# Half of the columns of two query-weight loads read from a source laid out in four spaced groups of 32 rows

## The chip, the cores and the metric

The kernel runs on one core of one Trainium2 chip. The metric is the device time of one execution in microseconds. A core has TensorE (PE in the profile; its weight loads are PEld), VectorE (DVE), ScalarE (ACT), GpSimd (POOL) and SyncE (SP). SP only issues transfers here. Sixteen DMA engines move the data between the device's memory (HBM) and the on-chip memory, SBUF, which has 128 partitions.

## The reference

The program is one decode step of a model with two layers, each an attention block and a token-mixing block, with the same weights and the same cache in both layers. All numbers are float32; the batch is 2, the width 512, with 32 query heads and 8 key/value heads of 128, and a cache of 32768 positions.

```python
B, Sq, D = 2, 1, 512
Hq, Hkv, Sk, Dh = 32, 8, 32768, 128
...
q = (x @ wq).reshape(B, Sq, Hq, Dh).transpose(0, 2, 1, 3)
scores = einsum("bhqd,bhkd->bhqk", q, repeat(k_cache, 4)) * Dh ** -0.5
o = einsum("bhqk,bhkd->bhqd", softmax(scores), repeat(v_cache, 4))
attention = o.transpose(0, 2, 1, 3).reshape(B, Sq, Hq * Dh) @ wo
...
x = x + attention(layernorm(x));  x = x + mixer(layernorm(x))     # layer 0
x = x + attention(layernorm(x));  x = x + mixer(layernorm(x))     # layer 1
```

The mixer is `w2` times gelu of `w1` times the normalised row, with a hidden size of 1792. The cache of one batch row and one key/value head is 16 MB of keys and 16 MB of values. There are 16 such pairs, and each is read once for each layer, except for a part that the kernel keeps between the layers.

## The kernel before

**Tiles.** `mem` is one large SBUF buffer, cut into 106 cells of 128 partitions x 512 columns (256 KB each). Keys, values and the weights `wq` and `wo` of a head all land in cells. A load fills 1 to 32 neighbouring cells; a weight load fills 4 cells (128 x 2048, 1024 KB).

**Units and steps.** A unit is (layer, batch row, head). It has a K phase of 64 cells (`k_step`, the products on L360, which make scores) and a V phase of 64 cells (`v_step`, L428, which makes the weighted sum of the values). A step is four cells. `Order` writes the order of all phases: K of one unit stands between V of the units before it, so that the softmax of a unit is done beside products of others. At the change of layers (twice, once for each batch row) the program has to finish a row's attention, its mixer and its normalisation before the first query of layer 1 for that row exists. Other units' phases fill that time. What lies before those two changes is the first long stretch (layer 0, to about 1000 us), and what lies behind them the second (layer 1, from about 1500 us).

**Queries.** `wide_products` (L325) multiplies the normalised rows with `wq` of one head, four products of 512 columns, one for each fourth of the 2048 columns of the load. `make_q` does this ten steps ahead of the unit's K phase. PE takes its instructions in one order, and a product that waits for its weights holds all that stand behind it.

**Loads.** `plan_loads` runs before the program is built. It walks the steps with estimated times, decides for each load how many cells it takes and which, and after which step SP issues it. A weight load for a query is asked for 16 steps ahead of its K phase. All loads of keys, values and weights are issued by SP, in one queue, in that order (L885 for keys and values, L880 for weights); SP waits until the products that read the cells' old content are done, and then issues. A transfer's landing is told by one of eight semaphores, taken in turn (DMAHW0 to DMAHW7 in the rows below); it counts to 16 when all parts of the transfer have landed. PE waits on that semaphore before it reads the cells. ACT issues two small loads at the start and one store of a single row of the output (L592); the last store (L757) is issued by SP.

**Sources.** The host lays the inputs out so that a load is 128 rows, one for each partition: `wqo[h]` has 128 rows, each with the 2048 columns of `wq` and then the 2048 of `wo`.

```python
part, layer, h = u
w = D * R
at_w = 0 if part == "q" else w
nc.sync.dma_start(cells(a, n), wqo[h][:, at_w : at_w + w])
```

Of the kernel before, what the change touches and what calls it, by code (L numbers as in the profile page):

```python
# [13 lines left out]
P = 128  # L14
# [24 lines left out]
STEP_US = 1.6  # L39
ASK_Q = 16  # L40
ASK_O = 8


class Order:
# [158 lines left out]


@with_exitstack
def gqa_mixer_kernel(ctx: ExitStack, tc: tile.TileContext, x, kt, v, wqo, cols, out):
    nc = tc.nc
    B, D = out.shape
    HKV = wqo.shape[0]
# [21 lines left out]
    def cells(a, n):  # L231
        return mem[:, a * G : (a + n) * G]
# [541 lines left out]
    for u in order.units:  # L774
        layer, b, h = u
# [11 lines left out]
    for name, us in users.items():  # L787
        k0 = min(first["K", u] for u in us)
        h = name if isinstance(name, int) else name[1]
# [3 lines left out]
        weights.append((k0 - ASK_Q if k0 else -1, ("q", layer, h), max(first["K", u] for u in us) if both else k0))  # L793
        weights.append((k0 if both else v0 + ASK_O, ("o", layer, h), max(end["V", u, 1] for u in us) + 3))

    for u in order.units:
        layer, b, h = u
# [76 lines left out]
    def load(label, n, a):  # L874
        kind, u, g = label
        if kind == "W":
            part, layer, h = u
            w = D * R
            at_w = 0 if part == "q" else w
            nc.sync.dma_start(cells(a, n), wqo[h][:, at_w : at_w + w])  # L880
            (wq_sb if part == "q" else wo_sb)[layer, h] = cells(a, n).rearrange("p (t c) -> p t c", t=DT)
            return
        layer, b, h = u
        src = (kt if kind == "K" else v)[b * HKV + h, g // HALF, :, (g % HALF) * G : (g % HALF + n) * G]
        nc.sync.dma_start(cells(a, n), src)  # L885
        for j in range(n):
            at_cell[kind, u, g + j] = a + j
            if (kind, u, g + j) in order.kept:
                at_cell[order.kept[kind, u, g + j]] = a + j
# [5 lines left out]
    for label, n, a in begin.get(-1, ()):  # L895
        load(label, n, a)
# [4 lines left out]
    for p, (kind, u, g) in enumerate(steps):  # L901
        (k_step if kind == "K" else v_step)(u, g)
        for f, args in hooks.pop(p, ()):
            f(*args)
        for label, n, a in begin.get(p, ()):
            load(label, n, a)
# [3 lines left out]
def _layout(A_x, A_k_cache, A_v_cache, A_wq, A_wo, B_w1, B_b1, B_w2, B_b2):  # L910
    import numpy as np

    B, HKV, SK, DH = A_k_cache.shape
    D = A_x.shape[-1]
    U = B * HKV
    kt = A_k_cache.reshape(U, 2, NG, 32, 2, 2, 8, 2, 2, DH).transpose(0, 1, 9, 4, 7, 8, 2, 5, 6, 3)
    wq = A_wq.reshape(D // P, P, HKV, -1).transpose(2, 1, 0, 3)
    wo = A_wo.reshape(HKV, -1, DH, D).transpose(0, 2, 1, 3)
    w1, b1, w2 = (a.reshape(P, -1) for a in (B_w1, B_b1, B_w2))
    none = np.zeros_like(w2)  # L920
    w2z = np.stack([none, w2], axis=2).reshape(P, -1)
    cols = [w1, b1, w2z, none[:, :1], np.broadcast_to(B_b2.reshape(1, 1), (P, 1))]
    return {
        "x": np.ascontiguousarray(A_x.reshape(B * (D // P), P).T),
        "kt": np.ascontiguousarray(kt).reshape(U, 2, DH, HALF * G),
        "v": A_v_cache.reshape(U, 2, P, HALF * G),
        "wqo": np.concatenate([wq.reshape(HKV, P, -1), wo.reshape(HKV, DH, -1)], axis=2),
        "cols": np.concatenate(cols, axis=1),
    }


_INS = ["x", "kt", "v", "wqo", "cols"]


# [20 lines left out]
```

## Time and profile before

| | |
|---|---|
| median of 3 runs | 2499.34 us (2498.99 to 2500.09) |
| the profiled execution's own time | 2498.83 us |
| its span in the trace | 2497.0 us |
| PE busy | 1339.3 us, 54% of the span |
| DVE, ACT, POOL busy | 211.4, 186.9 and 5.1 us |
| read from HBM | 1063.29 MB |
| mean rate of the DMA engines | 426 GB/s |
| SP's transfer queue (q1) | 99.1% of the time of 16 engines |

The span goes from the first instruction to the last; the execution's own time has some 2 us around it. The busy time of an engine is a sum over its instructions. The DMA row of the profile is a mean over 16 engines: 1.00 means that each of them had a packet under way at all times, and 0.50 that they were busy half of the time on average. PE waits for data for most of its idle time, so the question for any change here is which of the 16 engines ends last, and when.

### The profile page before, as it was taken

The numbers are of one execution on the slowest core, as the hardware profiler recorded it, in microseconds if no ns is written. First come the engines' busy times: TensorE is split into PE (matmuls) and PEld (weight loads), VectorE is DVE, ScalarE is ACT, GpSimd is POOL, SyncE is SP. The second block draws the span as 40 slices with busy tenths as digits, with TensorE's granted clock in tenths as the row PEclk, the third lists the DMA queues.
The fourth block names the chain that finished last, engine by engine and source line by source line (L and its number), as shares of the span: only waits on it lengthen the run. The fifth ranks groups of instructions, "written<-read, shape, count | busy, mean of one in ns | idle before, by whom it ended". The sixth has DMA issues, their size and how long they took to land.

```text
span 2497.0 us, 21065 instructions
## 1 busy us (share of the span) xinstructions
PE 1339.3 (54%) x9562; PEld 374.6 (15%) x9562; DVE 211.4 (8%) x600; ACT 186.9 (7%) x581; POOL 5.1 (0%) x18
## 2 busy tenths in 40 slices
PE   3445454444445544556676774554444544554567
PEld 1111111111111111111121221111111111111113
DVE  1000000000000000101110110000000000000012
ACT  0100000000000000001110210000000000000021
POOL 0000000000000000000000000000000000000000
PEclk8777777777777777778887986777777777777688
DMA  9999999999999999999999999999999999999996
GB/s 421 434 436 430 432 432 433 430 430 436 435 430 432 430 432 434 426 436 408 417 425 423 421 427 435 434 434 430 430 437 423 439 431 435 433 433 430 432 430 277
DMA packets 34947, 1064.64 MB, mean 426 GB/s; under 512 B 4134, under 2 KB 4138, under 8 KB 5035
## 3 DMA queue, kind: packets, MB, share of 16 engines
q1 hardware_dynamic: 34568, 1063.27, 99.1%
q8 instruction: 75, 1.23, 0.2%
q14 instruction: 14, 0.11, 0.0%
q10 hardware_dynamic: 290, 0.04, 0.0%
HBM read 1063.29 MB, written 0.00 MB: 426 GB/s over the span
## 4 chain that ended last, share of the span: by engine, by line
DMA 63%; PE 24%; another core or an unknown queue 11%; DVE 1%; issue 0%; ACT 0%; SPq 0%; POOLq 0%; POOL 0%; DVEq 0%; ACTq 0%
DMA mem<-in_v_dram 35%; DMA mem<-in_kt_dram 29%; PE acc L428 13%; PE scores L360 8%; PE misc L332 1%; PE bcast L325 0%; PE rows L492 0%; PE misc L384 0%; PE misc L657 0%; PE misc L451 0%; DVE row L462 0%; PE misc L378 0%; ACT S L410 0%; PE misc L471 0%
## 5 line engine op out<-in xcount | busy, mean ns | idle before, releaser
L428 PE MATMUL acc<-mem,S 128*16 128x512 f32 x4080 | 596.8, 719 | 586.9 <-DMA mem<-in_v_dram 578.6
L360 PE MATMUL scores<-mem,qz 128*32 128x512 f32 x4096 | 600.0, 727 | 538.4 <-DMA mem<-in_kt_dram 538.2
L410 ACT ACTIVATE S<-S,neg 128x128 f32<-128x128 f32 x256 | 129.6, 509 | 2213.8 <-DVE S L405 1188.7
L360 PEld LDWEIGHTS scores<-mem,qz 128*32 128x32 f32 x4096 | 142.5, 126 | 917.6 <-issue 827.0
L428 PEld LDWEIGHTS acc<-mem,S 128*16 128x16 f32 x4080 | 127.6, 107 | 903.5 <-issue 814.5
L370 DVE TENSOR_REDUCE mx<-scores 128x1 f32<-128x512 f32 x64 | 44.3, 691 | 801.3 <-PE scores L360 793.5
L405 DVE STREAM_TRANSPOSE S<-scores 128x512 f32<-128x512 f32 x64 | 45.5, 710 | 126.1 <-PE acc L428 126.1
L410 ACT ACTIVATION_READ_ACCUMULATOR S<-S,neg 128x1 f32 x256 | 47.7, 186 | 0.0
L492 PE MATMUL rows<-mem,oz 128*2 128x512 f32 x248 | 41.1, 744 | 0.3 <-DVE oz L481 0.3
L380 DVE TENSOR_REDUCE m<-misc 1x4 f32<-1x128 f32 x32 | 8.9, 279 | 380.8 <-PE misc L378 380.8
L453 DVE RECIPROCAL rl<-misc 128x4 f32<-128x4 f32 x32 | 5.8, 183 | 382.1 <-PE misc L451 382.1
L462 DVE SCALAR_TENSOR_TENSOR row<-acc,quad,row 128x128 f32<-128x128 f32 x96 | 33.6, 350 | 3.4
L460 DVE TENSOR_SCALAR row<-acc,quad 128x128 f32<-128x128 f32 x32 | 11.2, 351 | 170.3 <-PE acc L428 170.3
L481 DVE TENSOR_TENSOR oz<-misc,rl 128x4 f32<-128x4 f32 x32 | 5.2, 162 | 227.2 <-PE misc L471 226.7
L471 PEld LDWEIGHTS misc<-head,row 128*128 128x128 f32 x64 | 14.0, 274 | 52.2 <-issue 38.3
L325 PE MATMUL bcast<-mem,xw 128*32 128x512 f32 x144 | 20.0, 618 | 1.7 <-POOL x_rs L298 1.7
L471 PE MATMUL misc<-head,row 128*128 128x4 f32 x64 | 16.9, 334 | 7.3 <-DVE row L462 7.3
L451 PEld LDWEIGHTS misc<-both,one 128*128 128x128 f32 x64 | 12.9, 251 | 50.1 <-issue 47.2
L332 PEld LDWEIGHTS misc<-selg,row 128*128 128x128 f32 x128 | 17.1, 208 | 18.2 <-DVE rl L453 8.7
L576 ACT ACTIVATE row<-bcast,bias,scale 128x512 f32<-128x512 f32 x21 | 16.3, 777 | 37.8 <-PE rows L560 17.0
L378 PE MATMUL misc<-ident,mxa 128*1 128x128 f32 x64 | 18.1, 379 | 2.0 <-DVE mxa L376 2.0
L332 PE MATMUL misc<-selg,row 128*128 128x2 f32 (+1 forms) x128 | 18.5, 267 | 0.8 <-DVE row L317 0.8
(128 smaller groups left out, 278.1 us busy)
## 6 DMA issues: line engine op xcount, KB each, us to landing
mem<-in_v_dram SPq DMA_DIRECT2D x13, 4096.0 KB, 25.1
mem<-in_v_dram SPq DMA_DIRECT2D x37, 1024.0 KB, 9.1
mem<-in_kt_dram SPq DMA_DIRECT2D x15, 2048.0 KB, 17.9
mem<-in_kt_dram SPq DMA_DIRECT2D x30, 1024.0 KB, 10.3
mem<-in_wqo_dram SPq DMA_DIRECT2D x28, 1024.0 KB, 38.1
mem<-in_kt_dram SPq DMA_DIRECT2D x6, 4096.0 KB, 28.2
mem<-in_kt_dram SPq DMA_DIRECT2D x2, 6144.0 KB, 23.1
mem<-in_v_dram SPq DMA_DIRECT2D x3, 2048.0 KB, 38.8
```

Of the source, the lines that this page charges most:

```text
L325: nc.tensor.matmul(q_ps[us][32 * d : 32 * d + 32, :], xw[:, d, :], wq[:, d, :], start=True, stop=True)
L332: nc.tensor.matmul(pt[:, r * n : (r + 1) * n], q_row[us][:, r * DH : (r + 1) * DH], side, start=True, stop=True,)
L360: nc.tensor.matmul(sc_ps[u, half][32 * row : 32 * row + 32, :], qz[:, at : at + 32], cells(at_cell["K", u, g], 1), start=(i == 0), stop=(i ...
L370: nc.vector.tensor_reduce(mx[u][:, half : half + 1], sc_ps[u, half], axis=AX.X, op=ALU.max)
L378: nc.tensor.matmul(pm[:1, :P], mxa, ident, start=True, stop=True)
L405: nc.vector.transpose(S[half], sc_ps[u, half])
L410: nc.scalar.activation(s[:, :, h], s[:, :, h], AF.Exp, bias=neg[u][:, h : h + 1], scale=SCALE, accum_out=lsum[u][:, half, h : h + 1],)
L428: nc.tensor.matmul(acc[32 * row : 32 * row + R * QT, :], S[half][:, col : col + R * QT], vc, start=(g < NG), stop=(g >= quads - NG),)
L462: nc.vector.scalar_tensor_tensor(asb[u], acc[:, t * DH : (t + 1) * DH], quad[:, t : t + 1], asb[u], op0=ALU.mult, op1=ALU.add)
L471: nc.tensor.matmul(po_of[u][:, :R], asb[u], head, start=True, stop=(u != order.last))
L492: nc.tensor.matmul(rows[32 * r : 32 * r + B, :], oT[u][:, 2 * r + 1 - b : 2 * r + 3 - b], wo_of(u)[:, r, :], start=False, stop=(u == order ...
L576: nc.scalar.activation(hid[key, f], px[key], AF.Gelu_apprx_tanh, bias=shift[key][:, f : f + 1], scale=slope[key][:, f : f + 1],)
```

## The change

Two of the 28 weight loads are cut in two: `wq` of head 3 in layer 0 and `wq` of head 2 in layer 1. The left half (1024 of 2048 columns) is still read from `wqo`, as 128 rows. The right half is read from a new input, `narrow`. It holds the same numbers for each of the two loads, as four groups of 32 rows of 1024 columns, and behind each group stands one unused row of zeros, so that the four groups can't be written as 128 evenly spaced rows. The source pattern is then 4 groups x 32 rows x 1024 columns, and its slowest dimension is 4, where that of all other loads is 128. The destination is the right half of the columns of the same cells, 128 partitions. The bytes moved are the same, and no other load or instruction is changed.

```diff
+NARROW = (("q", 0, 3), ("q", 1, 2))
+NARROW_COLS = 1024
+NARROW_GROUPS = 4
...
-            nc.sync.dma_start(cells(a, n), wqo[h][:, at_w : at_w + w])
+            if u in NARROW:
+
+                cut = w - NARROW_COLS
+                nc.sync.dma_start(cells(a, n)[:, :cut], wqo[h][:, at_w : at_w + cut])
+                nc.sync.dma_start(cells(a, n)[:, cut:], narrow[NARROW.index(u)][:, : P // NARROW_GROUPS, :])
+            else:
+                nc.sync.dma_start(cells(a, n), wqo[h][:, at_w : at_w + w])
...
+    narrow = np.zeros((len(NARROW), NARROW_GROUPS, P // NARROW_GROUPS + 1, NARROW_COLS), np.float32)
+    for i, (part, _, h) in enumerate(NARROW):
+        w = (wq if part == "q" else wo)[h].reshape(NARROW_GROUPS, P // NARROW_GROUPS, -1)
+        narrow[i, :, :-1] = w[:, :, -NARROW_COLS:]
```

SP's queue at the first of the two loads, before. The names are the destination and the source, then the destination's sizes, and in brackets the semaphores that SP waits for ahead of the issue.

```order
L885 DMA mem<-in_kt_dram 128x16384 [waits DMAHW6_49,DMAHW1_49,PE_49]
L885 DMA mem<-in_kt_dram 128x16384 [waits DMAHW7_49,PE_49]
L880 DMA mem<-in_wqo_dram 128x2048 [waits DMAHW3_49]
L885 DMA mem<-in_v_dram 128x16384 [waits DMAHW0_49,PE_49]
L880 DMA mem<-in_wqo_dram 128x2048 [waits PE_49]
L885 DMA mem<-in_v_dram 128x16384 [waits DMAHW1_49,PE_49]
```

The same place after the change.

```order
L894 DMA mem<-in_kt_dram 128x16384 [waits DMAHW7_49,PE_49]
L886 DMA mem<-in_wqo_dram 128x1024 [waits DMAHW3_49]
L887 DMA mem<-in_narrow_dram 128x1x1024
L894 DMA mem<-in_v_dram 128x16384 [waits DMAHW0_49,PE_49]
L889 DMA mem<-in_wqo_dram 128x2048 [waits PE_49]
L894 DMA mem<-in_v_dram 128x16384 [waits DMAHW1_49,PE_49]
```

One row has become two, and the second waits for nothing of its own. The second load, `wq` of head 2 in layer 1, changes in the same way: it stands behind two loads of keys and ahead of a load of values there too. All loads behind the new one keep their order and take the next semaphore in turn.

PE at the products that read the first of these loads, before. In a row of L325 stand the products of the rows (`xw`) with the weights in `mem`, one for each fourth of the columns; `acc` is the weighted sum of values.

```order
L428 MATMUL acc<-mem,S_91 16x512 x12
L325 MATMUL bcast<-mem,xw 32x512 [waits DMAHW3_49]
L325 MATMUL bcast<-mem,xw 32x512 x3
L428 MATMUL acc<-mem,S_91 16x512 x4
L428 MATMUL acc<-mem,S_92 16x512 [waits DMAHW6_49,Activation_49]
```

The same place after the change.

```order
L431 MATMUL acc<-mem,S_91 16x512 x12
L328 MATMUL bcast<-mem,xw 32x512 [waits DMAHW3_49]
L328 MATMUL bcast<-mem,xw 32x512
L328 MATMUL bcast<-mem,xw 32x512 [waits DMAHW4_49]
L328 MATMUL bcast<-mem,xw 32x512
L431 MATMUL acc<-mem,S_91 16x512 x4
L431 MATMUL acc<-mem,S_92 16x512 [waits DMAHW7_49,Activation_49]
```

The last two of the four products now wait for the new transfer's own semaphore. DVE, ACT and POOL have the same rows as before.

More of the change, by code (lines that the diff above doesn't have):

```diff
@@ L205, in gqa_mixer_kernel @@
 @with_exitstack
-def gqa_mixer_kernel(ctx: ExitStack, tc: tile.TileContext, x, kt, v, wqo, cols, out):
+def gqa_mixer_kernel(ctx: ExitStack, tc: tile.TileContext, x, kt, v, wqo, narrow, cols, out):
     nc = tc.nc
@@ L927, in _layout @@
         "wqo": np.concatenate([wq.reshape(HKV, P, -1), wo.reshape(HKV, DH, -1)], axis=2),
+        "narrow": narrow,
         "cols": np.concatenate(cols, axis=1),
     }
-_INS = ["x", "kt", "v", "wqo", "cols"]
+_INS = ["x", "kt", "v", "wqo", "narrow", "cols"]
 def kernel(A_x, A_k_cache, A_v_cache, A_wq, A_wo, B_x, B_w1, B_b1, B_w2, B_b2):
```

## The prediction

> **What bounds the kernel now.** I read the page first: the DMA rows, the queues and the chain of waits.
>
> ```profile
> span 2497.0 us, 21065 instructions
> ...
> DMA  9999999999999999999999999999999999999996
> ...
> q1 hardware_dynamic: 34568, 1063.27, 99.1%
> q8 instruction: 75, 1.23, 0.2%
> ...
> DMA 63%; PE 24%; another core or an unknown queue 11%; DVE 1%; issue 0%; ACT 0%; SPq 0%; POOLq 0%; POOL 0%; DVEq 0%; ACTq 0%
> ```
>
> SP's queue (q1) fills 99.1% of the time of 16 engines. PE's 24% of the chain lies between landings, while the next loads are under way. So the kernel ends when the last DMA engine has moved its share, plus a tail. The second queue matters below: q8 carries the code of PE, 75 packets in 1.23 MB, so 16.4 KB each; 0.2% of 16 x 2497 us is 80 us, so about 1.07 us of one engine for each packet.
>
> The chain in order of time shows the end.
>
> ```profile
> 2398.86 41.45 DMA mem<-in_v_dram
> 2440.31 0.02 issue
> 2440.33 39.32 DMA mem<-in_v_dram
> 2479.65 0.04 issue
> 2479.70 0.45 PE held L437 x8
> ...
> 2493.94 0.35 DVE mem L756
> ```
>
> The last load of values lands at 2479.65 us and PE starts 0.05 us later. Behind it is a fixed tail of 17.4 us. Whatever the last landing gains or loses, the kernel gains or loses.
>
> Then the busy time by windows, for the two long stretches, the two changes of layer between them, and the last 14 us. The last two columns are the mean busy share of the 16 engines and their GB/s.
>
> ```profile
> 300.00:1000.00 700.00, 346.72 (x2411) 93.49 (x2412) 47.09 (x131) 35.88 (x136) 0.00 (x0) 0.73 1.00 432
> 1600.00:2400.00 800.00, 403.10 (x2830) 109.44 (x2822) 58.14 (x163) 51.94 (x174) 0.54 (x1) 0.75 1.00 433
> ...
> 1100.00:1260.00 160.00, 99.97 (x732) 28.13 (x736) 19.35 (x59) 24.79 (x60) 1.08 (x2) 0.84 0.99 415
> 1260.00:1480.00 220.00, 155.69 (x1170) 44.29 (x1166) 28.46 (x81) 26.86 (x68) 1.08 (x2) 0.84 1.01 425
> ...
> 2470.00:2472.00 2.00, 1.98 (x20) 0.67 (x24) 0.00 (x0) 0.00 (x0) 0.00 (x0) 1.00 1.01 414
> 2472.00:2474.00 2.00, 2.00 (x20) 0.60 (x12) 0.00 (x0) 0.00 (x0) 0.00 (x0) 1.00 0.66 268
> 2474.00:2476.00 2.00, 1.39 (x17) 0.40 (x17) 0.00 (x0) 0.00 (x0) 0.00 (x0) 1.00 0.49 205
> 2476.00:2478.00 2.00, 2.00 (x47) 1.41 (x40) 1.25 (x4) 0.00 (x0) 0.00 (x0) 1.00 0.50 198
> 2478.00:2480.00 2.00, 1.77 (x43) 0.85 (x35) 0.15 (x1) 0.00 (x0) 0.00 (x0) 1.00 0.19 69
> ```
>
> This is what to see: in the stretches all 16 engines work (1.00), but at the end the share falls to 0.66, stays at 0.5 for some 5 us and then goes to nothing. Half of the engines are done 5 to 7 us ahead of the other half. All have moved the same bytes of q1, since every large load is cut over 16 engines. Something else has held back eight.
>
> What it is, the completion marks tell: each transfer's semaphore is raised once by each engine. No view prints them; these are read from the trace behind the profile (issue, last mark, and how far ahead of it the other marks came, in us).
>
> ```
> issued    last mark   ahead of it by
>    2.12     65.27     1.9 1.8 1.7 1.6 1.6 1.6 1.6 1.6 1.5 1.5 1.5 1.4 1.4 1.1 1.0
>  358.34    405.82     3.6 3.3 3.2 3.1 2.8 2.7 2.7 2.3 1.8 1.8 1.8 1.7 1.6 1.5 0.1
>  943.07    973.09     6.7 6.3 6.3 5.8 5.6 5.3 5.2 4.4 1.8 1.7 1.7 1.7 1.6 1.5 0.1
> 1868.20   1916.77     3.8 3.6 3.5 3.5 3.3 3.0 2.8 2.7 1.4 1.3 0.5 0.3 0.3 0.3 0.1
> 2440.33   2479.65     7.1 6.9 6.8 6.8 6.6 6.3 5.3 5.1 1.7 0.8 0.6 0.6 0.5 0.4 0.3
> ```
>
> Eight engines run ahead more and more along a stretch, and lose part of that lead at the changes, where they run dry while the others work on. The other eight fall back one at a time, by about 1.5 us, and this happens at each packet of q8. So PE's code is fetched by eight of the engines in turn, and those eight end last.
>
> By the Trainium skill (Runtime: NRT & Kernel Launch, "Instruction fetch mechanics"), the code comes in blocks of 16 KiB through a DMA queue of the sequencer, and crossing a block is "mostly hidden". The block's size agrees with 16.4 KB a packet. That it is hidden does not hold for the engines that carry it: half of them are late by 5 to 7 us in the last windows.
>
> **The change part by part.** The unit price is 433 GB/s over 16, 27.1 GB/s an engine. A weight load of 1024 KB is 64 KB an engine, 2.42 us. If the new half goes over four engines, one of these two loads gives:
> - twelve engines 32 KB instead of 64: -1.21 us;
> - four engines 32 + 128 = 160 KB: +3.63 us.
>
> The rows are of 4 KB where they were 8 KB. The trace has no such long run of 4 KB rows. Bounds: nothing, or twice the loss that the first change of layer shows against the stretch with its rows of 8 KB (1 - 415/433, 4%), so 8%: 0.1 us on 32 KB and 0.5 us on 160 KB. I take the middle: -1.15 and +3.85 us.
>
> Now the question is which four. The engines that end last get -1.15 if they are not among them. The four then end last only where their lead is below 3.85 us. The one narrow transfer ahead of the end in this kernel is ACT's store of a single row:
>
> ```profile
> L592 ACTq DMA_DIRECT2D out_dram<-row x1: 505/505/505, 2409.3 to 2409.3; - x1
> ```
>
> Its packet of 2 KB, at 2413.84 us, stands in a gap of just one engine's packets in the trace, and that engine's marks are 6.6 us ahead. So the first engine that a narrow transfer takes is a leader. For the other three no row tells. By the Trainium skill (DMA: Bandwidth & Descriptors, "Why a DMA increments its semaphore by 16 and not by 1") a transfer runs on the largest number up to 16 that divides the slowest dimensions of both sides, here 4 of 4 and 128, and on the lowest-numbered engines. No view here shows those numbers.
>
> First stretch, if all four are leaders: right behind the load (marks at 405.82, leads of 2.3 to 3.6 us) they fall behind by up to 1.5 us. That costs nothing, because two more loads stand in their queues. Until 973 us they gain it back: of the eight leads seven are 5.2 or more and one is 4.4. The gain at the stretch's end is 1.15, or 4.4 - 3.85 = 0.55 if the slowest leader is among the four: I take 1.1 us. It goes through the changes whole, as the eight late engines have no idle time there (shares of 0.99 and 1.01, with the leaders' gaps in them). Second stretch: the smallest lead at the last landing is 5.1, more than 3.85, so the gain is 1.15 us.
>
> What the two products of L325 wait for is next. The load is issued right behind a load of keys, at both places:
>
> ```profile
> 358.34 0.33 SPq L885 DMA_DIRECT2D mem<-in_kt_dram  x1
> 358.72 0.42 SPq L880 DMA_DIRECT2D mem<-in_wqo_dram  x1
> 376.38 0.33 SPq L885 DMA_DIRECT2D mem<-in_v_dram  x1
> ...
> 358.34 47.48 DMA mem<-in_kt_dram
> ...
> 436.53 1.04 PE L325 MATMUL bcast<-mem,xw 128*32 128x512 f32 x8
> ...
> 1868.20 0.33 SPq L885 DMA_DIRECT2D mem<-in_kt_dram  x1
> 1868.58 0.42 SPq L880 DMA_DIRECT2D mem<-in_wqo_dram  x1
> 1887.83 0.33 SPq L885 DMA_DIRECT2D mem<-in_v_dram  x1
> ...
> 1868.20 48.56 DMA mem<-in_kt_dram
> ...
> 1948.18 1.04 PE L325 MATMUL bcast<-mem,xw 128*32 128x512 f32 x8
> ```
>
> The keys land at 405.82 and 1916.77, the weights 2.4 us later, and PE uses them at 436.53 and 1948.18: 28 and 29 us of cover for some 4 us. If that cover were gone, PE would stop at L325 with the values' products behind it. The second issue is 0.33 to 0.6 us more of SP; the next load is issued 17 us later, so nothing is pushed.
>
> Sum: -1.1 - 1.15 = -2.25 us. Against the profiled execution 2498.83 - 2.25 = 2496.6; it stands 0.5 us below the median of the runs, so I forecast 2499.34 - 2.25 = 2497.1 us, from 2496.2 to 2498.6 (one stretch's gain lost, or noise of half a us).
>
> **The rivals.** Slower: among the four are engines that fetch PE's code. Then each stretch ends on one of them, later by 3.85 less that engine's distance to the last (0 to 1.8 us in the marks of 973.09 and 2479.65). That is 2.05 to 3.85 a stretch, 4.1 to 7.7 together: 2503.4 to 2507.0, with 2505.3 as the middle. It decides as soon as one of the four leads by less than 3.85 us. For it: eight of 16 are late, and three of the four are not known. Against it: the store's engine leads by 6.6, and if the eight are one block, the four lie in the other.
>
> All engines alike: if a fetch cost its engine nothing, there would be no leaders, and the four would add 2 x 3.85 us: 2507.0. The 0.5 of the last windows speaks against it. This is what the "mostly hidden" of the Trainium skill (Runtime: NRT & Kernel Launch, "Instruction fetch mechanics") would make of it.
>
> The transfer is not narrow: with 128 partitions as destination it is cut over 16 engines all the same. Then one more issue and smaller rows remain, 0.1 us each: 2499.5. Against it: the source's slowest dimension is 4.
>
> More than the sum: in the changes the rate is 415 and 425 instead of 433, which is 160 x 18/433 + 220 x 8/433 = 10.7 us. If half of that comes from cells that wait for the late engines' landings, a smaller spread gives it back: 2497.1 - 5.4 = 2491.7. Against it: smaller rows alone can account for the lower rate.
>
> **How the numbers follow.** All four leaders 0.62; fetching engines among them 0.24; engines alike 0.02; not narrow 0.06; more than the sum 0.06. A change of 0.2% (5.0 us) is about what can be told from none here. The forecast and the case of no narrow transfer lie within it, and so do about 0.05 of the slower case; so 0.73 for within, 0.21 slower, 0.06 faster. The range goes from 2495.8, below the forecast's own end, to 2506.0 in the slower case, and leaves out about 0.06 below and 0.05 above.
>
> **What would show it.** Right: the share of 0.5 in the last windows starts later or is shorter, since four of the eight early engines end 3.85 + 1.15 = 5.0 us closer to the last; the last landing comes near 2477.4 instead of 2479.65; the chain has the same links. Wrong: PE waits at L328 for its weights; the share at the end is 0.2 or less for some us, so that a few engines end alone; or the windows at the end look as before, which would mean sixteen engines. The first number to fall would be the four engines' lead, which I have seen for one alone.

## The result, and the profile after

The changed kernel is slower: 2505.85 us median of 10 runs (2504.78 to 2508.63) beside 2499.05 us for 10 runs of the kernel before (2498.33 to 2500.09). The ratio is 1.0027, with an interval from 1.0019 to 1.0035. That is 6.8 us more, where the forecast was 2.25 us less. The profiled execution took 2505.02 us.

The page of the changed kernel, in the lines that answer to those shown of before (the row of GB/s has 40 slices of 62.6 us each):

```profile
span 2503.1 us, 21066 instructions
...
GB/s 419 435 434 432 431 433 406 432 433 428 432 431 436 432 433 434 424 433 416 420 428 425 417 430 439 432 430 432 435 433 400 435 433 431 434 434 430 432 433 278
...
q1 hardware_dynamic: 34832, 1063.27, 99.2%
q8 instruction: 75, 1.23, 0.2%
...
DMA 61%; PE 25%; another core or an unknown queue 13%; ACT 1%; DVE 1%; issue 0%; SPq 0%; POOLq 0%; POOL 0%; DVEq 0%; ACTq 0%
```

The bound is what it was: SP's queue fills 99.2% of the time of 16 engines, and the same bytes are moved. But outside the changes of layer two slices of the rate stick out, the 7th (375 to 438 us) with 406 GB/s and the 31st (1877 to 1940 us) with 400. These are where the two changed loads are transferred. A slice that is 62.6 us long and 27 or 33 GB/s below 433 has lost 3.9 or 4.8 us. The page of before has 433 and 423 in these two slices, so the second figure is partly the scatter of a slice.

The end of the chain of waits of the changed kernel (start, length, what):

```profile
2446.86 39.03 DMA mem<-in_v_dram
2485.89 0.04 issue
2485.94 0.45 PE held L440 x8
```

The last landing is at 2485.89 us, where it was at 2479.65: 6.24 us later. The tail behind it is 17.2 us, where it was 17.4. So the whole loss is in the transfers.

The windows of the changed kernel, the two long stretches and then the two changes of layer (the last two columns are the mean busy share of the 16 engines and GB/s):

```profile
300.00:1000.00 700.00, 343.36 (x2383) 91.99 (x2387) 47.26 (x132) 35.88 (x136) 0.00 (x0) 0.73 1.00 430
1600.00:2400.00 800.00, 403.02 (x2798) 108.60 (x2794) 57.46 (x162) 46.64 (x167) 0.54 (x1) 0.74 1.00 430
1100.00:1260.00 160.00, 102.88 (x740) 28.46 (x736) 19.50 (x59) 24.79 (x60) 1.09 (x2) 0.81 1.00 422
1260.00:1480.00 220.00, 155.25 (x1182) 43.85 (x1174) 28.46 (x81) 26.82 (x68) 1.08 (x2) 0.87 1.01 424
```

Both stretches went from 432 and 433 to 430 GB/s, with the engines as busy as ever (1.00). 2 of 432 over 700 us is 3.2 us, and 3 of 433 over 800 us is 5.5 us (the rates are rounded to 1 GB/s, so each figure is good to a microsecond or two). The engines were not idle; their packets took longer. The changes of layer have 422 and 424 GB/s where they had 415 and 425: nothing is lost there. And the last windows:

```profile
2476.00:2478.00 2.00, 2.00 (x24) 1.04 (x26) 0.00 (x0) 0.00 (x0) 0.00 (x0) 1.00 0.97 402
2478.00:2480.00 2.00, 2.00 (x23) 0.80 (x13) 0.00 (x0) 0.00 (x0) 0.00 (x0) 1.00 0.72 301
2480.00:2482.00 2.00, 1.37 (x15) 0.36 (x16) 0.00 (x0) 0.00 (x0) 0.00 (x0) 1.00 0.73 299
2482.00:2484.00 2.00, 2.00 (x39) 1.22 (x35) 1.03 (x3) 0.00 (x0) 0.00 (x0) 1.00 0.57 221
2484.00:2486.00 2.00, 1.76 (x49) 1.04 (x43) 0.37 (x2) 0.00 (x0) 0.00 (x0) 1.00 0.11 39
```

Before, the share was 0.5 for some 5 us and then went to nothing, since eight engines had ended ahead of the other eight. Now it stays near 1 until 2478 us and is 0.72 for 4 us after that: 12 of 16 engines. So four engines have left the leading group and end with the late ones. That is one of the signs named for the forecast. But all of it lies some 6 us later, and the landing of 2477.4 that was to go with it did not come.

The place where it is lost shows in windows of 2 us around the arrival of the first changed load, which SP issued at 357.67 (left half) and 358.15 us (right half):

```profile
404.00:406.00 2.00, 0.00 (x0) 0.00 (x0) 0.00 (x0) 0.00 (x0) 0.00 (x0) 0.50 1.28 324
406.00:408.00 2.00, 0.51 (x4) 0.23 (x8) 0.00 (x0) 0.00 (x0) 0.00 (x0) 0.50 0.90 213
408.00:410.00 2.00, 2.00 (x12) 0.45 (x8) 0.00 (x0) 0.00 (x0) 0.00 (x0) 0.50 1.35 328
410.00:412.00 2.00, 2.00 (x16) 0.67 (x12) 0.00 (x0) 0.00 (x0) 0.00 (x0) 0.50 0.76 213
412.00:414.00 2.00, 2.00 (x20) 0.54 (x16) 0.00 (x0) 0.00 (x0) 0.00 (x0) 0.89 0.96 356
414.00:416.00 2.00, 2.00 (x24) 0.58 (x20) 0.00 (x0) 0.00 (x0) 0.00 (x0) 1.00 0.77 328
```

The same stretch of time before the change:

```profile
404.00:406.00 2.00, 0.04 (x4) 0.07 (x7) 0.00 (x0) 0.00 (x0) 0.00 (x0) 0.50 1.22 516
406.00:408.00 2.00, 2.00 (x12) 0.61 (x16) 0.00 (x0) 0.00 (x0) 0.00 (x0) 0.50 1.31 565
408.00:410.00 2.00, 2.00 (x12) 0.45 (x8) 0.00 (x0) 0.00 (x0) 0.00 (x0) 0.50 0.98 426
410.00:412.00 2.00, 2.00 (x16) 0.59 (x12) 0.00 (x0) 0.00 (x0) 0.00 (x0) 0.62 0.86 369
```

A rate in windows this short scatters to both sides of 433, because a packet of 64 KB counts where it ends. But the six windows after the change have a mean of 294 GB/s, none above 356, at a mean share of 1.0: the engines hold packets under way all the time, and move two thirds of the bytes. The single packets in the trace say the same for every engine: one of 64 KB takes 2.42 us nearly everywhere else. Those that lie wholly within the slow stretch took 4.2 to 4.5 us, and they are packets of the twelve engines that carry nothing of the narrow transfer. One of 4 KB of the narrow transfer takes some 280 ns, where the first rows of the left half took 159. Added up, the packets took 4.2 us longer than their usual time in this place, as a mean of the 16 engines, and 4.1 us longer around 1924 us.

The completion marks of transfers, read from the trace of the changed kernel as those of before:

```
issued    last mark   ahead of it by
 357.29    407.35     5.0 4.8 4.6 4.4 4.3 4.3 4.0 3.6 3.4 3.4 3.3 3.3 3.2 3.1 0.1
 358.15    414.81     2.8 1.4 0.9            (the narrow transfer: four engines)
 947.36    977.21     7.4 7.1 7.1 6.4 3.2 3.1 3.1 3.1 3.0 2.9 2.8 2.0 1.1 1.1 1.0
2446.86   2485.89     8.2 8.0 7.7 7.4 3.0 2.3 2.3 2.3 2.3 1.9 1.8 1.7 1.3 1.0 0.8
```

At 977.21 there are three groups: four leaders, eight in the middle, and four last. The middle eight stand at 974.0 to 975.2 us, where the late eight of before stood at 971.3 to 973.1. That is 2.7 us later for the first of them and 2.1 for the last, where the forecast had them 1.15 earlier. The last four stand at 976.1 to 977.2.

### The profile page after: what moved, and what is told of

It is laid out like the page before. It is cut to its first block, busy times and chain, and to the rows that moved or that the text cites. A ratio compares the mean times of both kernels' runs of the same rounds, so it can differ in the third digit from the quotient of the medians.

```text
span 2503.1 us, 21066 instructions
## 1 busy us (share of the span) xinstructions
PE 1343.7 (54%) x9562; PEld 375.5 (15%) x9562; DVE 211.4 (8%) x600; ACT 186.9 (7%) x581; POOL 5.1 (0%) x18
## 3 DMA queue, kind: packets, MB, share of 16 engines
q1 hardware_dynamic: 34832, 1063.27, 99.2%
## 4 chain that ended last, share of the span: by engine, by line
DMA 61%; PE 25%; another core or an unknown queue 13%; ACT 1%; DVE 1%; issue 0%; SPq 0%; POOLq 0%; POOL 0%; DVEq 0%; ACTq 0%
DMA mem<-in_v_dram 35%; DMA mem<-in_kt_dram 26%; PE acc L431 14%; PE scores L363 8%; PE misc L335 1%; PE rows L495 0%; PE bcast L328 0%; PE misc L387 0%; PE misc L454 0%; PE misc L660 0%; SPq L894 0%; PE misc L474 0%; ACT S L413 0%; PE misc L381 0%
```

## The experiments

Two readings were to be told apart. The rival of the prediction: engines that fetch PE's code are among the four, so that late engines got the four's extra bytes (L in the expectations below). Against it, the reading A of the traces: while the narrow transfer runs, all 16 engines slow down. For A there were two causes to choose from. A1: an engine of the narrow transfer writes SBUF partitions that another engine writes in the ordinary loads, and this holds up both and whatever else shares the way. A2: the four streams of the narrow source read addresses in HBM that get in each other's way.

By the Trainium skill (DMA: Bandwidth & Descriptors, "The descriptor swizzle"), a transfer to 128 partitions gives each engine eight partitions of its own: engine 0 has 0 to 3 and 32 to 35, engine 1 has 4 to 7 and 36 to 39, and so on, with engines 8 to 15 on partitions 64 to 127. No view here prints which partition an engine writes, so the runs below test it by what a placement does to the rate. If each engine of a transfer in four groups of 32 rows takes one group, the first of them writes partitions 0 to 31, which by this table belong to eight engines.

**p1 and p2: shapes of a transfer, on the side.** Behind each of 12 weight loads an additional transfer from an input of ones goes into an unused tile `spare`. Two cells fewer are left for the loads. No work is left out. `d4`, `d16p` and their like are laid out as `narrow` is, with an unused row behind each group; `d4p` has rows of 16 KB, of which 4 KB are read.

```diff
-CELLS = 106
+CELLS = 104
+    spare = const.tile([P, 1024], F32, name="spare")
...
+        if kind == "k4":
+            go(spare, d4[:, :32, :])
+        if kind == "k16":
+            go(spare, d16)
+        if kind == "k16 spaced":
+            go(spare, d16p[:, :8, :])
+        if kind == "k4 pitch":
+            go(spare, d4p[:, :32, :1024])
...
+        if kind == "k4 own":
+            for e in range(4):
+                at = 32 * (e % 2)
+                c = 512 * (e // 2)
+                go(spare[at : at + 16, c : c + 512], d44[e, :, :4, :512])
+        if kind == "k4 far":
+            for e in range(4):
+                at = 64 + 32 * (e % 2)
+                c = 512 * (e // 2)
+                go(spare[at : at + 16, c : c + 512], d44[e, :, :4, :512])
...
             nc.sync.dma_start(cells(a, n), wqo[h][:, at_w : at_w + w])
+            probe(PROBE.get(u))
```

Expected of p1:

> The kernel before, with 104 cells instead of 106 and 4 KB a partition of spare memory that nothing reads; behind twelve weight loads an extra transfer into the spare memory is issued, of a different shape each. Nothing is left out. Theory A (the narrow transfer slows all engines while it runs): around the transfer of four groups of 32 rows the rate of the 16 engines falls from 433 to some 210 to 330 GB/s for about 8 us, at a busy share near 1, and the extra transfer of 128 plain rows shows no such fall (over 400). Within it, A1 (writes to partitions that another engine serves): the 16-row transfers to partitions 0 to 15 and 32 to 47 show no fall, those to 64 to 79 and 96 to 111 do, and the wider row pitch in the source changes nothing. A2 (addresses of the source): both 16-row places look alike, and the row pitch of 16 KB changes the fall. Theory L (only the four engines are late, the others run on): the rate stays above 400 at each of them until the share drops, and a 64 KB packet of the other engines keeps its 2.42 us. Time, by both: 12 extra transfers, some 5 MB or 12 us more than before, and by A 4 us for each of some six narrow ones besides: 2511 against 2535 us.

Expected of p2:

> As p1, with the shapes at other places, and one more: 16 groups of 8 rows, spaced, so that the pattern has a spaced slowest dimension but all 16 engines take part. A: each shape gives the same fall as in p1 wherever it stands; A3 (any spaced pattern is slow): the 16 spaced groups fall too, to 210 to 330 GB/s; by A1 and A2 they need not. L: no fall at any of them.

The times of both were missed: 2598.18 and 2577.07 us. The additional bytes went to a few engines over and over: if these are the same lowest-numbered ones each time, the first of them carries 1152 KB of these transfers in p1, which is 43.5 us at 2.42 us for 64 KB. The marks of p1's last landing lie up to 17 us apart, where those of before lay 7. How the 99 and 78 us come about stays open. So the totals say nothing of a single shape; the rates at each place do. Worked out from the packets of both traces, with a loss being the sum of 1 - rate/433 over windows of 1 us:

```
transfer                                    KB    us of rate lost
four groups of 32 rows (k4)                512    4.7, 4.4, 4.0
the same, rows 16 KB apart in HBM          512    4.7, 4.3
16 groups of 8 rows (k16 spaced)           512    3.1, 3.5
128 even rows (k16)                        512    none at three places
four engines, partitions 64-79, 96-111     128    1.7, 1.5, 1.5
four engines, partitions 0-15, 32-47       128    none at three places
```

Eight groups of 16 rows, and four transfers to 32 partitions each, lost 2.9 us or more as well. The last two rows are transfers of the same shape, on four engines, of the same source, and differ only in the partitions they write. Their windows in p1, first into 0-15 and 32-47 (arriving at 446.9 to 451.0 us, the three windows around it):

```profile
444.00:448.00 4.00, 0.13 (x4) 0.16 (x8) 0.00 (x0) 0.00 (x0) 0.00 (x0) 0.50 0.98 421
448.00:452.00 4.00, 4.00 (x29) 1.09 (x28) 0.28 (x1) 0.00 (x0) 0.00 (x0) 0.64 1.12 480
452.00:456.00 4.00, 4.00 (x39) 1.18 (x35) 0.16 (x1) 0.00 (x0) 0.00 (x0) 1.00 0.95 410
```

and into 64-79 and 96-111 (615.5 to 622.3 us):

```profile
612.00:616.00 4.00, 0.00 (x0) 0.00 (x0) 0.00 (x0) 0.00 (x0) 0.00 (x0) 0.50 0.90 370
616.00:620.00 4.00, 3.00 (x16) 0.69 (x17) 0.00 (x0) 0.00 (x0) 0.00 (x0) 0.50 1.02 294
620.00:624.00 4.00, 4.00 (x32) 1.49 (x31) 0.44 (x2) 0.00 (x0) 0.00 (x0) 0.80 1.07 422
```

The first three have a mean of 437 GB/s. Of the second, the window in the middle has 294 at a share of 1.02: there the packets of 64 KB of the twelve other engines took 3.5 to 3.8 us. So A2 falls: the distance of the rows in HBM changes nothing (4.7 and 4.7 in p1), and the same source costs 1.5 us or nothing by where it is written. A1 stands. And four engines are no condition for it: 16 groups of 8 rows, on 16 engines, lose 3.1 to 3.5 us, while 128 even rows, which by the table give each engine the same partitions as in an ordinary load, lose nothing.

The two places differ in one more way: 0-15 and 32-47 lie in the lower half of the partitions, 64-79 and 96-111 in the upper. The four transfers to 32 partitions each, which go from the lowest partitions up, tell these apart. In p2 the first engine has done the second of them (partitions 32 to 63) at 583.5 us by its mark. So nothing of them was written above partition 63 before that, and yet 64 KB packets of other engines that ended between 582.2 and 583.5 us had taken 2.9 to 3.3 us. So the slowing is not one of the upper half alone.

**t_wide: the change with 128 even rows as its source.** The split, the additional issue, the rows of 4 KB and the other input stay; only the grouping goes.

```diff
-                nc.sync.dma_start(cells(a, n)[:, cut:], narrow[NARROW.index(u)][:, : P // NARROW_GROUPS, :])
+                nc.sync.dma_start(cells(a, n)[:, cut:], narrow[NARROW.index(u)])
```

> The changed kernel with the new source as 128 plain rows, so that both halves of the two loads go over all 16 engines. Both theories: the loss is gone, 2499.3 us (2498.5 to 2500), and the rate near 405 and 1920 us stays over 400 GB/s. If the loss stays (2505), it comes from the second input or the cut in two, and both theories fall.

Measured: 2498.87 us beside 2498.95 for the kernel before; ratio 1.0000 [0.9991, 1.0009]. The windows at the same place:

```profile
404.00:406.00 2.00, 0.03 (x4) 0.06 (x5) 0.00 (x0) 0.00 (x0) 0.00 (x0) 0.50 1.29 537
406.00:408.00 2.00, 2.00 (x12) 0.61 (x16) 0.00 (x0) 0.00 (x0) 0.00 (x0) 0.50 1.31 561
408.00:410.00 2.00, 2.00 (x16) 0.49 (x12) 0.00 (x0) 0.00 (x0) 0.00 (x0) 0.72 0.91 393
410.00:412.00 2.00, 2.00 (x24) 0.67 (x20) 0.00 (x0) 0.00 (x0) 0.00 (x0) 1.00 0.94 401
```

They go up and down as before, with a mean of 473 GB/s where those of before have 469. So the additional issue, the smaller rows and the second input cost nothing that can be measured, and the whole loss hangs on the grouping.

**t_first: the first of the two loads alone.**

```diff
-NARROW = (("q", 0, 3), ("q", 1, 2))
+NARROW = (("q", 0, 3),)
```

> The changed kernel with the first of the two loads alone (layer 0, head 3). A: half of the loss, 3.4 us, so 2502.4 us (2501.8 to 2503.2), since each event costs by itself. L: one stretch's loss of 2.05 to 3.85 us, 2501.1 to 2502.9; told from A by the packets near 405 us: 4.2 us for 64 KB by A, 2.42 us by L.

Measured: 2502.04 us, ratio 1.0013 [1.0004, 1.0022]: 3.1 us, a little under half of the change's 6.8. The time fits A and L alike; the packets decide, as 64 KB take up to 4.4 us near 405 us. The windows around the first load and around the place of the second:

```profile
404.00:406.00 2.00, 0.00 (x0) 0.00 (x0) 0.00 (x0) 0.00 (x0) 0.00 (x0) 0.50 1.29 352
406.00:408.00 2.00, 0.98 (x8) 0.39 (x12) 0.00 (x0) 0.00 (x0) 0.00 (x0) 0.50 1.03 244
408.00:410.00 2.00, 2.00 (x16) 0.52 (x12) 0.00 (x0) 0.00 (x0) 0.00 (x0) 0.50 1.17 287
410.00:412.00 2.00, 2.00 (x12) 0.45 (x8) 0.00 (x0) 0.00 (x0) 0.00 (x0) 0.50 0.86 244
1920.00:1922.00 2.00, 2.00 (x16) 0.65 (x12) 0.00 (x0) 0.00 (x0) 0.00 (x0) 0.50 1.20 516
1922.00:1924.00 2.00, 2.00 (x16) 0.51 (x11) 0.00 (x0) 0.00 (x0) 0.00 (x0) 0.50 1.21 524
```

The rate falls at the first place and not at the second. The streams of packets in this trace also tell which engines the four are: each of the four that carry narrow packets is one of the eight that lead. The trace of the change says the same near 1916 us, where eight engines' marks lie 1.5 us or more ahead of all others and the four are among these eight. By the end of t_first the four have made up what they carried: the marks of the last landing (2481.95) are again 4.4 to 6.8 us ahead for eight engines and within 1.2 us for the other eight. What stays is the late eight's share, 2481.95 - 2479.65 = 2.3 us. With the 1.15 us of bytes that they were spared, about 3.5 us of slowing have come through to the end. The packets near 405 us lost 3.7 us or more on each engine in this trace; where the small rest went stays open.

**t_16: 16 groups of 8 rows instead of four groups of 32.** All 16 engines now carry the same share, so that no engine gets more bytes than before.

```diff
-NARROW_GROUPS = 4
+NARROW_GROUPS = 16
```

> The changed kernel with 16 spaced groups of 8 rows instead of 4 groups of 32: all 16 engines get equal shares, as before, but engine i writes partitions 8i to 8i+7 and not the ones that it writes in all other loads. A1 (writes to partitions that another engine serves slow everything while they last): a fall to some 250 GB/s for 8 us at each of the two loads, 3.1 to 3.5 us each as in the probe, so 2505.4 us (2504.5 to 2506.5), though no engine has more to move than before. L (four engines get too much): no loss, 2499.0 us.

Measured: 2504.9 us beside 2498.92, ratio 1.0024 [1.0015, 1.0033]. Its windows at the first load, and at the end:

```profile
404.00:406.00 2.00, 0.00 (x0) 0.00 (x0) 0.00 (x0) 0.00 (x0) 0.00 (x0) 0.50 1.65 401
406.00:408.00 2.00, 0.99 (x8) 0.39 (x12) 0.00 (x0) 0.00 (x0) 0.00 (x0) 0.50 1.17 305
408.00:410.00 2.00, 2.00 (x16) 0.52 (x12) 0.00 (x0) 0.00 (x0) 0.00 (x0) 0.50 0.82 268
410.00:412.00 2.00, 2.00 (x16) 0.52 (x12) 0.00 (x0) 0.00 (x0) 0.00 (x0) 0.68 0.79 328
```

```profile
2480.00:2482.00 2.00, 1.24 (x16) 0.46 (x12) 0.00 (x0) 0.00 (x0) 0.00 (x0) 1.00 0.61 250
2482.00:2484.00 2.00, 2.00 (x20) 0.64 (x14) 0.14 (x1) 0.00 (x0) 0.00 (x0) 1.00 0.47 195
2484.00:2486.00 2.00, 2.00 (x51) 1.59 (x53) 1.26 (x4) 0.00 (x0) 0.00 (x0) 1.00 0.49 189
2486.00:2488.00 2.00, 1.35 (x34) 0.60 (x22) 0.29 (x1) 0.00 (x0) 0.00 (x0) 1.00 0.04 13
```

The rate falls to 268 to 401 GB/s in the four windows, with no engine overloaded. At the end the share of about 0.5 is back, for about as long as before; the last landing is 7.2 us later in this execution (2506.42 us, one of the two longest of eleven). In the packets of this trace the rate lost is 3.0 and 3.1 us at the two loads, and the median is 6.0 us above that of before. Nothing was moved from one engine to another, and the loss is nearly that of the change. So the loss doesn't need four engines that get more than others. By A1 it comes from the partitions that the engines write.

**b2 and b3: only partitions that belong to the engines, on eight engines.** By that table of the Trainium skill (DMA: Bandwidth & Descriptors, "The descriptor swizzle") engines 0 to 7 write partitions 0 to 63 in a wide load; what follows agrees with it. Here all of a changed `wq` load goes into partitions 0 to 63 of eight cells, in two transfers of eight groups of four rows of 16 KB, and VectorE copies one half to partitions 64 to 127. b3 does it for a third load (layer 1, head 5). The planner reserves eight cells for such a load.

```diff
+                for e in range(2):
+                    nc.sync.dma_start(cells(a, n)[32 * e : 32 * e + 32], narrow[NARROW.index(u), e][:, :4, :])
...
+        nc.vector.tensor_copy(cells(a, WCELLS)[P // 2 :], cells(a + WCELLS, WCELLS)[: P // 2])
```

> The kernel before, with the same two loads (layer 0 head 3, layer 1 head 2) moved by eight engines that write only partitions they serve in all other loads: partitions 0 to 63 take their own rows and beside them the rows of partitions 64 to 127, as two transfers of 32 partitions in 8 spaced groups of 4 rows, and VectorE copies the second part up to partitions 64 to 127 some 10 us ahead of its use. A1, with engines 0 to 7 as the leaders: no fall of the rate; the late engines have 2.42 us less to move in each stretch, the leaders 2.42 more, which their lead of 4.4 to 7.1 covers: a gain of 2.0 to 2.4 a stretch, 2494.4 us (2494 to 2495.2). If A1 is wrong and any spaced narrow transfer slows all: 2502 or more. If some of engines 4 to 7 fetch PE's code: 2.42 us later for them in each stretch less up to 1.8, so 2500.5 to 2503.8, with no fall of the rate.

> As b2, with a third load so moved, for layer 1 head 5, near 1428 us at the end of the changes of layer, where the marks of the kernel before show the leaders only 2.0 to 2.5 us ahead. A1: if the leaders' idle time in the changes is what is used, another 2.4 us, 2492.1; if the lead of 2.0 to 2.5 is all there is, the leaders become the late ones for a while and regain it before the next load, since a fetch costs the late ones 1.5 us each 300 us: no gain beside b2, 2494.4, or up to 2.4 us worse where the third load lands late (2496.8).

Measured: b2 2503.44 us, ratio 1.0017 [1.0009, 1.0026]; b3 2506.31 us, ratio 1.0029 [1.0018, 1.0041]. Both forecasts by A1, of a gain, were missed by 9 us and more. b2 lies where its third case has it (some of engines 4 to 7 fetch PE's code), and also above the 2502 of its second (any spaced narrow transfer slows all). The packets decide between these: the slowing is gone, 64 KB packets take their 2.42 us near the load, and the rows of 16 KB 611 ns. The loss has another shape, in the last windows of b2:

```profile
2478.00:2480.00 2.00, 1.48 (x17) 0.51 (x19) 0.00 (x0) 0.00 (x0) 0.00 (x0) 1.00 0.24 95
2480.00:2482.00 2.00, 2.00 (x39) 1.15 (x34) 0.88 (x3) 0.00 (x0) 0.00 (x0) 1.00 0.13 51
2482.00:2484.00 2.00, 1.81 (x49) 1.10 (x39) 0.52 (x2) 0.00 (x0) 0.00 (x0) 1.00 0.12 39
```

The share is 0.24, then 0.13 and 0.12: two engines end alone, for some 4 us. At the first load, the marks of b2 show what these are: of its eight engines six were leaders, and two were late ones already. So, by the numbers of that table, two of the eight engines that fetch PE's code lie in the lower half, and they got 128 KB of such a load instead of 64, on top of their fetches. Here the mechanism of the prediction's slower rival is at work, though not in the change. b3, with one more such load, loses 2.9 us more.

**b4: the change's own split on the four engines, into partitions that are their own.** The left half comes as in the change. The right half goes to partitions 0 to 15 and 32 to 47 of eight spare cells, as two transfers of four groups of four rows (4096 columns each). Four selecting products of PE for each half of it and a copy by VectorE bring the rows to their place. The bytes of each engine and the order in SP's queue are those of the change. SP issues the right half later (391.67 instead of 358.15 us, and 1886.26 instead of 1872.69), but the first load's packets reach the engines at the same place, from 403.1 us.

```diff
+                nc.sync.dma_start(cells(a, n)[:, : w // 2], wqo[h][:, at_w : at_w + w // 2])
+                for e in range(2):
+                    nc.sync.dma_start(
+                        cells(a + WCELLS, 2 * WCELLS)[32 * e : 32 * e + 16], narrow[NARROW.index(u), e][:, :4, :]
+                    )
...
+        for s in range(4):
+            nc.tensor.matmul(
+                got[32 * s : 32 * s + 32, :],
+                put[:48, :],
+                cells(a + WCELLS + 2 * s + half, 1)[:48, :],
...
+        nc.vector.tensor_copy(cells(a + 2 + half, 1), got)
```

> The two loads with the change's own split (32 KB an engine over all 16, then 128 KB on each of the four lowest), but without a write to a partition that another engine serves: the second half of the columns goes as 2 transfers of 16 partitions (0 to 15 and 32 to 47), 4 spaced groups of 4 rows, into spare cells beside the load; eight products of PE with a 48 x 32 selection and two copies by VectorE put the rows into their 128 partitions some 10 us ahead of their use. This is the prediction's sum without the slowing: -2.25 us, 2496.7 us (2495.8 to 2497.6), with the rate at 433 GB/s near both loads and the four among the engines that end within a microsecond or two of the last. If the four hold engines that fetch PE's code: 2.05 to 3.85 us a stretch, 2503 to 2506.6. If any spaced transfer slows all: 2505.5.

Measured: 2497.78 us (2496.61 to 2499.91) beside 2498.85, ratio 0.9994 [0.9985, 1.0003]. The windows at the first load:

```profile
404.00:406.00 2.00, 0.00 (x0) 0.01 (x1) 0.00 (x0) 0.00 (x0) 0.00 (x0) 0.50 1.09 463
406.00:408.00 2.00, 1.98 (x12) 0.67 (x16) 0.00 (x0) 0.00 (x0) 0.00 (x0) 0.50 1.01 436
408.00:410.00 2.00, 2.00 (x12) 0.45 (x8) 0.00 (x0) 0.00 (x0) 0.00 (x0) 0.50 1.14 492
410.00:412.00 2.00, 2.00 (x20) 0.63 (x16) 0.00 (x0) 0.00 (x0) 0.00 (x0) 0.78 0.96 401
```

They have a mean of 448 GB/s; the place where the change has 270 in the same four windows is gone. With the same bytes on each engine, b4 is 8 us faster than the change (2497.78 against 2505.85). That it is the partitions is argued from the lost slowing, since the row widths, the products of PE, the reserved cells and the time of issue differ from the change as well. In its trace (2499.91 us, the longest of the eleven) four engines' marks lie 6.0 us or more ahead of the last landing and twelve within 2.9, so four leaders have joined the late ones, as the prediction had it. That the gain is the forecast's is not shown: -1.1 us is on its side, half of its -2.25 and just outside its range, and can't be told from none. It isn't a version that beats the kernel before by anything measurable, and why half is missing stays open.

## Why the prediction was wrong, step by step

- **The bound and the tail.** Right. The last landing sets the end, and the tail is 17.2 us where 17.4 were read.
- **Eight engines fetch PE's code and end last.** Right, and it explains b2 and b3 as well. By the end windows of t_16 and the marks of t_first, half of the engines still end some 4 to 7 us ahead.
- **Twelve engines -1.15 us, four engines +3.85 us a load.** This is the step that failed. It priced the narrow transfer by its bytes and by 27.1 GB/s an engine, with at most 8% for rows of 4 KB, and took the other engines' rate as given. The runs show a term that is missing from the sum: while such a transfer runs, all 16 engines slow down, by a mean of 4.1 to 4.2 us a load. The late eight come out at 2.1 to 2.7 us later instead of 1.15 earlier, and the four, with 4 KB packets at some 280 ns instead of about 159, at some 9 us later at the end of the first stretch instead of 3.85 (by the groups of marks, which don't name engines). The bounds were taken from rows of ordinary loads, none of which, by A1, writes the partitions of other engines; so the trace of before held no row for it, and the text should have said so and put the missing cost in as a rival.
- **The four are leaders.** Right: the streams of t_first and of the change show it for all four, where the prediction had one.
- **28 to 29 us of cover for the products' weights.** Right: the narrow half landed at 414.81 us and PE read it at 443.68, without a wait of its own; its products take 0.86 us in the chain.
- **The additional issue and the smaller rows cost next to nothing.** Right; t_wide is that kernel, at 1.0000.
- **The sum.** The late eight alone, at about -1.15 + 3.5 = +2.35 us a load with the 3.5 that t_first leaves, would give +4.7 us. With the 4.1 to 4.2 us that the packets lost they would give some 6. The last landing moved by 6.24. That the last 1 or 2 us are the four, which are the last at 977.21 and end among the twelve that land within 3.0 us, fits, but the marks don't name engines: it is argued and not shown.
- **The rivals.** The slower one gave 2503.4 to 2507.0 us and the kernel took 2505.85. But its mechanism is not what happened: no engine among the four fetches code, and t_16 loses nearly as much with no engine loaded more than another. The size agrees by accident. "Engines alike" and "not narrow" are refuted by the marks; "more than the sum" finds nothing for it in b4, where the spread of the engines is smaller by four leaders: the gain is 1.1 us, 3.7 at the end of its interval, where that rival has 7.6.

## What to carry to other kernels

Before bytes are moved from late DMA engines to early ones, look at which partitions each engine will write. By the runs here, a grouped source is best read as giving each engine a block of neighbouring partitions instead of the set that it has in a load of 128 even rows; no view prints the partitions. In four or sixteen groups, 512 KB of it cost this kernel 3 to 4.7 us of the rate of all 16 engines. And where the trace of before has no row for a transfer's shape, price the other engines' loss as an unknown with both signs, or measure that shape beside the kernel first.

## What was not expected of the hardware

All 16 engines slowed, and not just those whose partitions were crossed. In the case of partitions 64-79 and 96-111, the crossed partitions would by the same table of the Trainium skill belong to engines 8 to 11. But 64 KB packets of all twelve other engines took 3.5 to 3.8 us instead of 2.42. By the Trainium skill (DMA: Bandwidth & Descriptors, "Back-pressure in remote DMA"), a saturated destination port of SBUF clogs the way back to the source engines and to other engines that share that way. It says so of transfers between cores; what is seen here would go with it inside one core, but no run shows the way itself, so why all engines slow stays open.

A load of four groups raised its semaphore by four marks of engines, one of 16 groups by 16, so a grouping decides how many engines carry a transfer, and the equal spread over 16 was no protection. Two groups of 64 rows (k2) were the worst shape: 512 KB took 5.9 us of rate at one place and 14.4 at another. What makes the difference between these two stays open.
